# A planned order of 840 tasks is written anew, two more blocks of y are turned by DMA, and the idle matmuls multiply zeros by zeros

## The chip, the cores and the metric

The kernel runs on one core of a Trainium2 chip. The metric is the device time of one execution in microseconds (us). Lower is better. All times in this document are device times or times inside a profiled execution, counted from the start of its span.

## The reference

The program is a gated linear recurrence followed by a two-layer network with a SiLU. Four sequences of 768 steps with 8 heads of width 48 go through the recurrence. Its output, 3072 rows of 384, goes through a 384 x 2048 matrix, SiLU and a 2048 x 384 matrix.

```python
f = 1.0 / (1.0 + np.exp(-f_logit))
for t in range(S):                                   # S = 768
    state = f[:, :, t, :, None] * state + np.einsum('bhd,bhe->bhde', k[:, :, t], v[:, :, t])
    y[:, :, t] = np.einsum('bhd,bhde->bhe', q[:, :, t], state)
x = y.transpose(0, 2, 1, 3).reshape(B * S, H * D)    # 3072 x 384
h = x @ w_in                                         # w_in 384 x 2048
out = (h / (1.0 + np.exp(-h))) @ w_out               # w_out 2048 x 384
```

## The kernel before

A sequence is cut into six chunks of 128 steps, so that there are 24 blocks (sequence, chunk). `PAIRS` joins them into twelve pairs, numbered 0 to 11, each with two blocks, 0 and 1. Pairs 0 to 3 (kind 'T') hold the first two chunks of one sequence, interleaved by step. Pairs 4 to 11 (kind 'N') hold the same chunk of two sequences. A chunk needs the state that the chunk before it left.

The work on a pair is split into small tasks. A task has a kind, a pair and mostly a block, so `sc.7.0` is the score task of block 0 of pair 7:

- `f`, `k`, `q`, `v` load a pair's inputs. `wi` and `wo` (four of each, on the POOL queue) load a quarter of the first and the second matrix, lines 206 and 209.
- `E` and `L` make the logarithm of the gate on ACT, `cs` sums it over the steps by matmul (lines 304 to 314), `ia`, `a` and `al` take exponentials of the sums (line 316 and its neighbours), and `ki` and `qg` multiply k and q by them (line 321).
- `tq` turns the products on the tensor engine (line 328), and `qkc` copies them out of PSUM. In pairs 4 to 11 `qkD` does both by a transposing DMA on the SP queue (line 336).
- `sc` makes the scores (lines 345, 349), `at` masks them (line 353), `y` applies them to v and adds the state's part (lines 262, 361, 365), `yi` is the state's part alone in block 1 of a 'T' pair.
- `d`, `sd` and `su` (lines 274 or 382, 386, 392) carry the state forward. `vb` casts v.
- `yc` copies y out of PSUM. Then `yT` turns it by three matmuls with an identity (line 373) and `xc` copies the result into the tile xT. Or `yD` does both by one transposing DMA on the SP queue (line 377).
- `mi` (line 248) is one eighth of the first matrix product for a pair, six matmuls of width 256. `si` (line 253) is the SiLU of it. `mo` (line 285) is a quarter of the second product for a block, four matmuls of width 384. `oc` copies the result out of PSUM, `so` stores it.

There is no scheduler at build time. The text `PLAN` is a table of about 840 words, made by a planner outside the kernel; the kernel issues the tasks in the order of the words. A word is `task:engine:buffers`. The engine is A (ACT, the scalar engine), V (DVE, the vector engine), G (POOL), S (the SP queue) or P (the tensor engine, PE). The buffers are the numbers of the tiles that the task opens, out of `SLOTS`: eight PSUM banks `pb`, four `f`, six each of `k`, `q`, `v`, and so on. So the table fixes, for each engine, the order in which it takes its instructions; what an engine waits for follows from the data and from the buffers. An engine stands still at an instruction whose inputs are not there, and everything behind it stands too. The SP queue is such an engine as well: nearly all DMAs are issued by it in the order of the table.

Words `idle.W.n` are n matmuls of width W whose result nobody reads; they fill the tensor engine's time in the opening. The first four loads of the table are issued ahead of everything else, before the constants are made. ACT has two tables of functions, one for exponentials and logarithms, one for SiLU, and a table is loaded (line 484) wherever the table of tasks changes from one to the other.

Of the kernel before, what the change touches and what calls it, by code (L numbers as in the profile page):

```python
# [43 lines left out]
v.0.0:S:4 d.1:P:2,7 at.1.0.0:V: idle.512.5::3 y.1:P:4,3 qg.0.0:G: qg.0.1:V:2 wi.0:G: L.2.0:A:1 tq.0.0:P:6 q.2.0:S:4 k.2.0:S:3 cs.2.0:P:5 ki.0.1:V:
sd.1.0:A:0 tq.0.1:P:2 al.0:A:0 su.1.0:G:0 cs.2.1:P:1 yc.1.0:A:2 yT.1.0:P:0 qkc.0.0:V:0 qkc.0.1:V: ia.2.0:A:1 xc.1.0:V:3 yi.1.1:P: a.2.0:A:4 wi.2:G:
vb.0.0:V:1 sc.0.1:P:2,4 v.2.0:S:5 a.2.1:A:0 yc.1.1:A:0 vb.0.1:G:3 al.2:A:4 idle.256.1::6 yT.1.1:P:6 ia.2.1:A:2 sc.0.0:P:5,1 d.0:P:3,0 at.0.1.1:V:1
at.0.1.0:V: xc.1.1:A: mi.1.2:P:4 at.0.0.1:V:2 mi.1.3:P:6 at.0.0.0:V: y.0:P:5,1 yc.0.0:V:2 sd.0.0:A:0 su.0.0:G:0 yi.0.1:P: wo.0:G: wo.1:G: mi.1.6:P:2
si.1.3:A:0 f.3.0:S:3 sd.1.1:V:1 yc.0.1:A:1 yT.0.0:P:5 yT.0.1:P:6 xc.0.1:V:1 mi.1.7:P:3 xc.0.0:A: si.1.7:A: si.1.2:A: sd.0.1:V:0 f.5.0:S:2 si.1.6:A:
mi.0.3:P:5 mi.0.0:P:0 mi.0.2:P:7 mi.0.7:P:4 mi.0.1:P:6 mi.1.4:P:1 mi.1.5:P:3 si.1.4:A: si.0.1:A:1 ki.2.0:V:1 mi.0.5:P:2 si.0.0:A: mi.1.0:P:6 si.0.5:A:
mi.0.4:P:0 mi.1.1:P:1 si.1.5:A: si.0.2:A: si.1.0:A: si.1.1:A: mo.0.1.0:P:2 mo.0.0.0:P:3 wo.2:G: mo.1.0.0:P:7 mi.0.6:P:6 si.0.6:A: mo.1.1.0:P:1  # L50
si.0.3:A: si.0.7:A: ki.2.1:G:4 mo.1.0.1:P: qg.2.1:V: qg.2.0:V: mo.1.1.1:P: mo.0.1.1:P: tq.2.0:P:4 qkc.2.0:V:1 tq.2.1:P:6 mo.0.0.1:P: wo.3:G: si.0.4:A:
qkc.2.1:V: mo.1.1.2:P: sc.2.1:P:6,4 sc.2.0:P:0,5 at.2.0.0:V:0 at.2.0.1:V: mo.1.0.2:P: mo.0.0.2:P: at.2.1.0:V:1 at.2.1.1:V: mo.0.1.2:P: mo.0.1.3:P:
vb.2.0:G:0 vb.2.1:A:1 d.2:P:6,5 su.0.1:G:0 sd.2.0:V:0 y.2:P:4,0 mo.1.1.3:P: oc.0.1:V:0 mo.0.0.3:P: E.3.0:A:1 L.3.0:A:1 cs.3.0:P:2 yc.2.0:V:1 E.5.0:A:0
L.5.0:A:0 a.3.0:A:4 su.2.0:G:0 sd.2.1:V:0 q.5.0:S:0 yi.2.1:P: yc.2.1:A:0 yT.2.0:P:4 cs.3.1:P:6 al.3:A:0 ia.3.1:A:1 cs.5.0:P:5 xc.2.0:V:0 a.5.0:A:0
cs.5.1:P:0 k.3.0:S:0 ki.3.1:G:0 yT.2.1:P:4 xc.2.1:V: oc.0.0:A:1 q.3.0:S:1 mo.1.0.3:P: oc.1.0:A:2 oc.1.1:V:3 qg.3.0:V:1 mi.2.6:P:4 al.5.1:A:2
qg.5.0:V:2 k.5.1:S:1 a.5.1:A:1 mi.2.0:P:1 mi.2.1:P:7 mi.2.2:P:3 q.5.1:S: qg.5.1:V:3 ia.5.1:A:2 al.5.0:A:3 a.3.1:A:4 qg.3.1:V: k.5.0:S: ia.5.0:A:0
# [51 lines left out]
def kernel(  # L108
# [32 lines left out]
    buf = {}  # L141
# [290 lines left out]
    def run(kind, rest, eng, got):  # L432
        if kind == "idle":
            for _ in range(rest[1]):
                nc.tensor.matmul(buf["pb", int(got)][:, 0:rest[0]], triu, zero[:, 0:rest[0]], start=True, stop=True, skip_group_check=True)  # L435
            return
# [80 lines left out]
```

## Time and profile before

| | us |
|---|---|
| median of three runs | 181.32 |
| the three runs | 177.69, 181.32, 600.86 |
| the profiled execution, its own time | 175.95 |
| its span in the trace | 174.2 |
| outside the span | 1.75 |
| PE busy in the span | 168.2 (97%) |
| ACT busy | 128.6 (74%) |
| DVE busy | 81.5 (47%) |
| POOL busy | 63.4 (36%) |

The busy time of an engine is the time in which an instruction of its own runs, without waiting, branching or issuing of DMAs. The ends of matmuls are modelled. The granted clock of the tensor engine stands at full in all slices. DMA shares are the mean over 16 DMA engines of the time that packets took, and they can be above one in a short stretch. A chain of waits is followed back from the last instruction to what released it.

### The profile page before, as it was taken

To read this page: it belongs to the slowest core of one execution; us is meant where nothing else is said; L and a number is where in the kernel's file an instruction comes from. 1 tells how busy PE (TensorE), PEld (TensorE's weight loads), DVE (VectorE), ACT (ScalarE), POOL (GpSimd) and SP (SyncE) were. 2 spreads that over 40 slices of the span, in tenths; PEclk is the share of its full clock that TensorE was granted. 3 is DMA by queue.
4 is the path that set the end of the run, shared out by engine and by line. 5 is a ranking of instruction groups with operands and counts; after the bars stand their busy time and mean duration, and the time that the engine had idled before them with its cause. 6 is when DMAs were issued, how large, how long until landed. Compare 5 with 4: busy or idle time off the path is not lost.

```text
span 174.2 us, 4746 instructions
## 1 busy us (share of the span) xinstructions
PE 168.2 (97%) x1927; PEld 125.2 (72%) x1927; DVE 81.5 (47%) x166; ACT 128.6 (74%) x237; POOL 63.4 (36%) x106
## 2 busy tenths in 40 slices
PE   6889999999999999999999999999999999999992
PEld 2456888666876888766787687786697686886872
DVE  7389713267858762126686176045760152520101
ACT  3879839665999989997499688999589574281630
POOL 6088612312583357400737235400470970000000
PEclk9999999999999999999999999999999999999999
DMA  5999999999899998999999895969979998222202
GB/s 143 323 322 210 214 224 204 229 184 263 191 202 182 213 198 179 222 191 212 177 222 177 162 224 131 221 133 226 224 145 186 202 198 226 49 72 108 90 4 90
DMA packets 110677, 32.12 MB, mean 184 GB/s; under 512 B 104096, under 2 KB 110528, under 8 KB 110656
## 3 DMA queue, kind: packets, MB, share of 16 engines
q1 hardware_dynamic: 106048, 27.76, 75.7%
q0 software_dynamic: 3936, 3.74, 12.1%
q10 hardware_dynamic: 672, 0.33, 0.6%
q8 instruction: 15, 0.25, 0.6%
q14 instruction: 6, 0.05, 0.1%
HBM read 25.17 MB, written 4.72 MB: 172 GB/s over the span
## 4 chain that ended last, share of the span: by engine, by line
PE 85%; ACT 7%; DVE 2%; DMA 2%; issue 1%; ACTq 0%
PE pb L285 35%; PE pb L248 32%; ACT hT L253 3%; PE pb L349 3%; ACT L484 2%; PE pb L361 2%; PE pb L328 2%; DMA f<-in_f_logit_dram 2%; PE pb L365 2%; PE pb L373 2%; PE pb L311 2%; PE pb L345 1%; ACT x L316 1%; PE pb L382 1%; PE pb L262 1%; DVE atm L353 1%
## 5 line engine op out<-in xcount | busy, mean ns | idle before, releaser
L248 PE MATMUL pb<-xT,w_in_sb 128*128 128x256 bf16 x576 | 69.5, 272 | 0.2 <-ACT hT L253 0.2
L285 PE MATMUL pb<-w_out_sb,hT 128*128 128x384 bf16 (+2 forms) x400 | 68.7, 320 | 0.0
L248 PEld LDWEIGHTS <-w_in_sb 128*128 128x128 bf16 x576 | 54.7, 98 | 9.1 <-issue 0.7
L253 ACT ACTIVATE hT<-pb 128x512 bf16<-128x512 f32 x96 | 50.5, 609 | 14.4 <-PE pb L248 14.1
L285 PEld LDWEIGHTS <-hT 128*128 128x128 bf16 x400 | 37.2, 98 | 20.3
L392 POOL TENSOR_TENSOR st<-sd,al 48x192 bf16<-48x192 f32 x40 | 21.9, 549 | 48.4 <-PE pb L361 34.1
L316 ACT ACTIVATE x<-pb 128x384 f32<-128x384 f32 x48 | 21.4, 499 | 5.8 <-PE pb L304 2.5
L353 DVE TENSOR_TENSOR atm<-pb,triu 128x512 bf16<-128x512 f32 x32 | 20.1, 684 | 11.2 <-PE pb L349 6.6
L484 ACT ACT_TABLE_LOAD x17 | 21.8, 1283 | 0.3
L183 DVE COPY ob<-pb 128x384 f32<-128x384 f32 (+1 forms) x11 | 5.7, 528 | 27.3 <-PE pb L285 27.3
L321 POOL TENSOR_TENSOR qk<-k,x 128x384 bf16<-128x384 f32 x12 | 13.0, 1094 | 12.8 <-DMA k<-in_k_dram 9.7
L386 DVE TENSOR_TENSOR sd<-pb,st 128x384 f32<-128x384 f32 x16 | 8.8, 552 | 11.5 <-PE pb L382 10.6
L321 POOL TENSOR_TENSOR qk<-q,x 128x384 bf16<-128x384 f32 x11 | 10.9, 997 | 8.5 <-ACT x L316 7.9
L233 ACT ACTIVATE e<-f 128x768 f32<-128x768 f32 x12 | 10.1, 842 | 3.8 <-DMA f<-in_f_logit_dram 3.7
L181 ACT COPY ob<-pb 128x384 f32<-128x384 f32 (+1 forms) x14 | 6.7, 476 | 8.3 <-PE pb L285 8.1
L321 DVE TENSOR_TENSOR qk<-q,x 128x384 bf16<-128x384 f32 x13 | 9.0, 710 | 5.8 <-ACT x L316 5.7
L321 DVE TENSOR_TENSOR qk<-k,x 128x384 bf16<-128x384 f32 x12 | 8.0, 677 | 6.7 <-DMA k<-in_k_dram 6.6
L353 DVE TENSOR_TENSOR atm<-pb,mask 128x512 bf16<-128x512 f32 x16 | 10.0, 684 | 1.6 <-PE pb L345 1.6
L183 DVE CAST yb<-pb 128x384 bf16<-128x384 f32 x13 | 7.1, 555 | 6.7 <-ACT hT L253 3.1
L183 POOL CAST vb<-v 128x384 bf16<-128x384 f32 x13 | 7.0, 542 | 8.4 <-DMA v<-in_v_dram 8.0
L435 PE MATMUL pb<-zero,triu 128*128 128x512 bf16 (+1 forms) x26 | 7.5, 424 | 1.4 <-POOL triu masks.py:66 1.4
L181 ACT CAST yb<-pb 128x384 bf16<-128x384 f32 x11 | 5.3, 488 | 4.3 <-PE pb L365 4.3
(70 smaller groups left out, 138.9 us busy)
## 6 DMA issues: line engine op xcount, KB each, us to landing
f<-in_f_logit_dram SPq DMA_DIRECT2D x11, 384.0 KB, 5.5
k<-in_k_dram SPq DMA_DIRECT2D x10, 384.0 KB, 5.5
q<-in_q_dram SPq DMA_DIRECT2D x10, 384.0 KB, 4.6
v<-in_v_dram SPq DMA_DIRECT2D x10, 384.0 KB, 5.0
out_dram<-ob SPq DMA_DIRECT2D x13, 192.0 KB, 2.1
w_in_sb<-in_moe_w_in_dram POOLq DMA_DIRECT2D x4, 384.0 KB, 8.7
w_out_sb<-in_moe_w_out_dram POOLq DMA_DIRECT2D x4, 384.0 KB, 9.7
out_dram<-ob SPq DMA_DIRECT2D x14, 96.0 KB, 3.4
```

The costliest lines, as they stand in the source:

```text
L181: nc.scalar.copy(dst, src)
L183: ENG[eng].tensor_copy(dst, src)
L233: return nc.scalar.activation(e, at("f", P)[:, j * w:(j + 1) * w], AF.Exp, scale=-1.0)
L248: nc.tensor.matmul(h[:, i, cols], w_in_sb[:, kk, n * 128:(n + 1) * 128], at("xT", P)[:, kk, cols], start=(kk == 0), stop=(kk == KT - 1))
L253: return nc.scalar.activation(at("hT", P)[:, 2 * j:2 * j + 2, :], at("h", P, j).rearrange("p (n c) -> p n c", n=2), AF.Silu)
L285: nc.tensor.matmul(at("o" + key, P, i)[:, 0:cols.stop - cols.start], at("hT", P)[:, n, i * C:(i + 1) * C], w_out_sb[:, n, cols], start=(n ...
L316: nc.scalar.activation(at(kind, P, i).rearrange("p h d -> p (h d)"), at("cs", P, i)[:, 0:HD], AF.Exp, scale=1.0 if kind == "ia" else -1.0)
L321: ENG[eng].tensor_mul(at("qk", P, i)[:, j, :, 0:D], heads("qk"[j], P, i), at("ia" if j else "a", P, i))
L353: ENG[eng].tensor_mul(at("atm", P, i)[:, r], at(f"s{r}", P, i).rearrange("p (n c) -> p n c", c=C), mask[:, None, :].to_broadcast([C, NP, C]))
L386: nc.vector.tensor_add(at("sd", P, i), d_ps, prev_state(P, i))
L392: nc.gpsimd.tensor_mul(at("st", P, i)[lo:lo + D, :, r * D:(r + 1) * D], at("sd", P, i)[lo:lo + D, :, r * D:(r + 1) * D], al_of(P, i)[lo:lo ...
L484: nc.scalar.preload_act_table_set(turns[n])
```

## The change

Three things are changed, and nothing else in the kernel.

1. `PLAN` is a new table. The same tasks stand in a new order, on partly other engines and in other buffers. The planner that wrote it counts fetches of instructions when it estimates when transfers land. Of the two ways to turn y, 13 blocks take `yT` where 15 did, and 11 take `yD` where 9 did: blocks `6.1` and `9.1` go over from `yT` and `xc` to `yD`.
2. The idle matmuls read the tile `zero` as both operands. Before, the stationary operand was the triangle `triu`, which POOL makes; `zero` is filled by DVE.
3. Of the `idle` words, the second run of width 512 has four matmuls in place of five, and a third run of five has become one. The rest stand in about the same places.

```diff
-f.1.0:S:0 k.1.0:S:4 idle.512.10::4 q.1.0:S:1 f.0.0:S:1 f.1.1:A: E.1.0:A:0 L.1.0:A:0 idle.512.1::0 idle.256.1::0 cs.1.0:P:6 a.1.0:A:2 cs.1.1:P:0
+f.1.0:S:3 k.1.0:S:3 q.1.0:S:1 f.1.1:A: f.0.0:S:0 idle.512.10::7 E.1.0:A:0 L.1.0:A:2 idle.512.1::0 idle.256.1::0 cs.1.0:P:4 a.1.0:A:1 v.1.0:S:3
...
-                nc.tensor.matmul(buf["pb", int(got)][:, 0:rest[0]], triu, zero[:, 0:rest[0]], start=True, stop=True, skip_group_check=True)
+                nc.tensor.matmul(buf["pb", int(got)][:, 0:rest[0]], zero[:, 0:C], zero[:, 0:rest[0]], start=True, stop=True, skip_group_check=True)
```

The new order is shown at three places, by the instructions that stand in a row on an engine.

The first place is POOL in the opening, from the third and fourth quarter of `w_in` on. `qk...<-q` is `qg`, `qk...<-k` is `ki`, `st` is `su`, and `w_out_sb` is `wo`. Before:

```order
L206 DMA w_in_sb_161<-in_moe_w_in_dram 128x3x512
L183 CAST vb3_101<-v4_81 128x384
L392 TENSOR_TENSOR st00_148<-sd0_126,al0_128 48x4x48 x2
L209 DMA w_out_sb_162<-in_moe_w_out_dram 128x4x384 x3
L321 TENSOR_TENSOR qk4_97<-k3_68,x2_90 128x8x48
L209 DMA w_out_sb_162<-in_moe_w_out_dram 128x4x384
```

And now:

```order
L183 CAST vb2_100<-v1_78 128x384
L206 DMA w_in_sb_161<-in_moe_w_in_dram 128x3x512
L392 TENSOR_TENSOR st00_148<-sd1_127,al3_131 48x4x48 x2
L209 DMA w_out_sb_162<-in_moe_w_out_dram 128x4x384
L392 TENSOR_TENSOR st10_149<-sd0_126,al4_132 48x4x48 x2
L321 TENSOR_TENSOR qk1_94<-q2_73,x0_88 128x8x48
L209 DMA w_out_sb_162<-in_moe_w_out_dram 128x4x384 x2
L321 TENSOR_TENSOR qk2_95<-q2_73,x4_92 128x8x48
L321 TENSOR_TENSOR qk2_95<-k3_68,x1_89 128x8x48
L209 DMA w_out_sb_162<-in_moe_w_out_dram 128x4x384
```

The second and third quarter of `w_out` were issued right behind the first; now they stand behind `su.1.1` and `qg.2.0`, and `qg.2.0` waits for the load `q.2.0`. The last quarter of `w_in` has moved behind a cast that waits for `v.0.0`.

The second place is the SP queue around the transposes of pairs 6 and 7. `qkT` is `qkD`, `xT` is `yD`. Before:

```order
L227 DMA f0_61<-in_f_logit_dram 128x16x48
L296 DMA out_0_dram<-ob3_137 64x384 x2
L336 DMA_TRANSPOSE qkT0_105<-qk3_96 128x8x128
L377 DMA_TRANSPOSE xT1_119<-yb1_116 128x3x128
L336 DMA_TRANSPOSE qkT2_107<-qk1_94 128x8x128
L227 DMA k1_66<-in_k_dram 128x16x48
```

And now:

```order
L227 DMA f2_63<-in_f_logit_dram 128x16x48
L296 DMA out_0_dram<-ob1_135 64x384 x2
L336 DMA_TRANSPOSE qkT3_108<-qk2_95 128x8x128
L336 DMA_TRANSPOSE qkT2_107<-qk1_94 128x8x128
L377 DMA_TRANSPOSE xT0_118<-yb2_117 128x3x128
L377 DMA_TRANSPOSE xT0_118<-yb0_115 128x3x128
L227 DMA k5_70<-in_k_dram 128x16x48
```

The two `qkD` of pair 7 now follow each other, and both `yD` of pair 6 stand behind them, where one `yD` stood between them.

The third place is PE ahead of the scores of pair 7 (line 349). Line 285 is `mo`, 311 `cs`, 382 `d`, 248 `mi`. Before:

```order
L285 MATMUL pb0_140<-w_out_sb_162,hT1_123 128x384
...
L311 MATMUL pb4_144<-lf0_85,triu_152 128x384
...
L382 MATMUL pb1_141<-vb2_100,qk1_94 128x96
...
L311 MATMUL pb6_146<-lf0_85,triu_152 128x384
...
L285 MATMUL pb3_143<-w_out_sb_162,hT1_123 128x384
...
L248 MATMUL pb1_141<-xT1_119,w_in_sb_161 128x256
...
L349 MATMUL pb0_140<-qkT0_105 128x128
```

And now:

```order
L285 MATMUL pb2_142<-w_out_sb_162,hT1_123 128x384
L311 MATMUL pb4_144<-lf2_87,triu_152 128x384
...
L382 MATMUL pb0_140<-vb3_101,qk2_95 128x96
...
L349 MATMUL pb7_147<-qkT3_108 128x128
...
L349 MATMUL pb5_145<-qkT2_107 128x128
...
L285 MATMUL pb2_142<-w_out_sb_162,hT1_123 128x384
```

`cs.8.1`, `d.7.1`, the last quarter of `mo.4.1` and the first `mi` of pair 6 stood ahead of the scores of pair 7; now the scores come first.

More of the change, by code (lines that the diff above doesn't have):

```diff
@@ L44 @@
[L44 to L55, printed above, removed]
@@ new lines @@
+mi.2.6:P:7 ki.3.1:V: al.5.0:A:4 al.5.1:A:2 ia.5.1:A:4 ki.3.0:V: tq.3.1:P:5 tq.3.0:P:3 mi.2.7:P:6 f.4.0:S:2 si.2.1:A:0 si.2.0:A: ki.5.1:V:4 mi.2.2:P:1
+v.5.1:S:5 qg.5.0:V:3 qkc.3.0:V:1 qkc.3.1:V: mi.2.5:P:3 si.2.4:A: si.2.6:A: si.2.3:A: si.2.5:A: mo.2.1.0:P:5 d.3:P:0,2 sc.3.1:P:4,3 ki.5.0:V: si.2.2:A:
+at.3.1.0:V:1 sc.3.0:P:7,1 qkD.5.0:S:2 si.2.7:A: at.3.0.1:V:0 qg.5.1:G: at.3.1.1:V: sd.3.0:A:0 mo.2.1.1:P: qkD.5.1:S:3 mo.2.1.2:P: mo.2.1.3:P:
+mo.2.0.0:P:0 mo.2.0.1:P: v.5.0:S: E.6.0:A:0 su.3.0:G:0 sd.3.1:V:0 oc.2.1:V:5 at.3.0.0:V: E.4.0:A:1 L.4.0:A:0 sc.5.0:P:5,3 L.6.0:A:1 su.0.1:G:0
```

110 lines of the change are left out of this document (59 added, 51 removed).

## The prediction

> **What bounds the kernel now.** First the page: the span, how busy the engines are, and the chain that ended last.
>
> ```profile
> span 174.2 us, 4746 instructions
> PE 168.2 (97%) x1927; PEld 125.2 (72%) x1927; DVE 81.5 (47%) x166; ACT 128.6 (74%) x237; POOL 63.4 (36%) x106
> PE 85%; ACT 7%; DVE 2%; DMA 2%; issue 1%; ACTq 0%
> ```
>
> The tensor engine (PE) is busy nearly throughout and carries 85% of the chain. Where it is not, the view by stretches of time tells.
>
> ```profile
> core 0: us, PE busy (x) PEld busy (x) DVE busy (x) ACT busy (x) POOL busy (x), PEclk, DMA share, GB/s
> 0.00:18.20 18.20, 15.55 (x233) 9.25 (x234) 13.41 (x44) 13.02 (x26) 10.59 (x29) 1.00 1.03 248
> 18.20:62.00 43.80, 43.77 (x598) 33.49 (x595) 25.25 (x45) 34.58 (x67) 16.95 (x26) 1.00 1.10 208
> 62.00:74.00 12.00, 11.83 (x105) 9.79 (x103) 3.33 (x8) 11.77 (x21) 7.51 (x10) 1.00 1.02 209
> 74.00:150.00 76.00, 76.00 (x808) 56.04 (x806) 35.46 (x65) 59.24 (x105) 28.37 (x41) 1.00 0.94 189
> 150.00:171.10 21.10, 21.08 (x195) 16.59 (x193) 3.79 (x7) 10.02 (x19) 0.00 (x0) 1.00 0.18 57
> ```
>
> Three things are to be seen. From 18.2 us to 171.1 us PE stands still for 0.03 + 0.17 + 0.02 = 0.22 us in all, so a new order finds almost nothing there to remove. In the opening, PE is idle for 2.65 us and otherwise holds filler, so an order could win there. And the DMA engines are as full as PE until 150 us (shares 0.94 to 1.10): the loads keep pace with PE, but not by much. So PE's work sets the end, and DMA is a second limit close behind.
>
> **The opening, 0 to 18.2 us.** In the chain of waits it is a ladder over three engines:
>
> ```profile
> 7.61 1.51 DVE qk L321 x3
> 9.17 0.64 PE pb L328 x8
> 9.83 0.70 DVE qkTT L183
> 10.57 0.44 PE pb L345 x16
> 13.58 0.57 PE pb L262 x32
> 14.71 0.33 PE pb L304 x2
> 18.25 1.42 PE pb L248 x12
> L183 DVE CAST vb<-v 128x384 bf16<-128x384 f32 x6 | 2.5, 428 | 8.0 <-DMA v<-in_v_dram 8.0
> ```
>
> The new table puts `vb.1.0` on DVE between the two `qkc` of pair 1, so the copy at 9.83, the scores at 10.57 and `y` at 13.58 come up to 0.43 us later (one such cast, mean 428 ns). `al.1` leaves the place ahead of the exponentials on ACT, which wins under 0.1 us. `cs.2.0`, which stood behind `y.1` (14.71, 0.33 us), goes ahead of it, into time in which PE only filled. So the first `mi` (18.25) moves by +0.43 - 0.1 - 0.33 = 0.0 us. Five idle matmuls fewer cost or win nothing: they stood in such waits. Zeros for both operands let the filler start before the triangle is ready, but the first real matmul waits for the gate's load and logarithm whenever the filler starts. The bounds for the opening are -1.7 us (two thirds of the 2.65 us idle) and +0.5 us (the cast is paid whole and a little more).
>
> ACT loads two more tables in the new order (one exponential now stands between the first SiLUs):
>
> ```profile
> L484 ACT ACT_TABLE_LOAD x17 | 21.8, 1283 | 0.3
> L253 ACT ACTIVATE hT<-pb 128x512 bf16<-128x512 f32 x96 | 50.5, 609 | 14.4 <-PE pb L248 14.1
> ```
>
> That is 2 x 1.283 = 2.6 us of ACT at about 22 us. It is hidden as long as PE finds free PSUM banks, since the SiLUs wait 14.1 us in all for PE, not PE for them. Without that cover it would cost at most 1 us, as eight banks let PE run on for some `mi` first. I take nothing.
>
> **The weights on POOL.** `wo.1` and `wo.2` now stand behind `qg.2.0`, and that waits for `q.2.0`:
>
> ```profile
> 10.18 1.29 SPq L227 DMA_DIRECT2D q<-in_q_dram  x1
> DMA to landing us min/median/max: 3.5/6.9/12.8
> L321 POOL TENSOR_TENSOR qk<-q,x 128x384 bf16<-128x384 f32 x11 | 10.9, 997 | 8.5 <-ACT x L316 7.9
> 19.95 2.29 POOL L209 DMA_DIRECT2D w_out_sb<-in_moe_w_out_dram  x3
> DMA to landing us min/median/max: 7.8/9.7/13.3
> 21.52 7.92 PE pb L248 x72
> 32.05 2.60 PE pb L285 x16
> ```
>
> (The landing rows are of `q` from 8 to 40 us, and of `w_out_sb`.) By the longest landing `q.2.0` is there at 10.18 + 12.8 = 23.0, `qg.2.0` ends at 24.0, and `wo.1` is issued then, where it was issued at 20.7. It lands at 31.8, 33.7 or 37.3 by shortest, median and longest. PE needs it at the first second-quarter `mo`: from 18.25 on there stand 16 `mi` (0.66 each, 7.92/12), four `mo` (0.65, 2.60/4), and about 2.1 us of one `y` (0.57 at 13.58), two `tq` (0.64 at 9.17) and smaller ones, which makes 33.5. By the median that is a wait of 0.2 us, and I take that; the bounds are 0 and 3.8 us. For the low end speaks that `wo.0`, issued ahead of it as before, keeps the POOL queue's transfers going meanwhile, so that `wo.1` need not land later than it did. What is queued behind the waiting `qg.2.0` on POOL is exactly `wo.1`, `wo.2`, `qg.2.1` and `ki.2.1`.
>
> **Two blocks of y by DMA.** Three transposes of a block take this on PE:
>
> ```profile
> 93.25 0.17 PE pb L373 x3
> ```
>
> Two blocks are 0.34 us of PE, which is on the path, so -0.34 us; their copies were on engines with slack. The Trainium skill (TensorE: Matmul & The Clock Gate, Part 4) gives about 275 ns for one transpose within a kernel; by that figure six would be 1.65 us. The row shows them pipelined at 0.06 us each, and the row decides. What replaces them is a transposing DMA on SP each, and the time that this needs before `mi` can start:
>
> ```profile
> 92.39 1.61 SPq L336 DMA_TRANSPOSE qkT<-qk  x1
> 94.12 1.19 SPq L377 DMA_TRANSPOSE xT<-yb  x1
> 95.40 1.25 SPq L336 DMA_TRANSPOSE qkT<-qk  x1
> DMA to landing us min/median/max: 3.1/3.6/5.4
> DMA to landing us min/median/max: 2.3/2.3/4.2
> 99.32 0.82 PE L248 MATMUL pb<-xT,w_in_sb 128*128 128x256 bf16 x6
> 100.07 0.62 PE L349 MATMUL pb<-qkT 48*128 48x128 bf16 x16
> ```
>
> (The first landing row is that of `qkT`, the second that of `xT`.) This is the place in the new order that is tightest. Now, the second `qkD` of pair 7 is issued at 95.40 and lands at 99.0 by the median, 1.1 us ahead of the scores at 100.07. In the new order it goes ahead of the `yD`, so it is issued at about 94.12 and lands at 97.7. But PE arrives earlier too: one `mo` quarter (0.65), one `mi` (0.66), and a `cs`, a `d` and a `yT` (0.6 together, an estimate by the row of 0.17) no longer stand ahead, 1.9 us, so it is there at 98.15, or 97.9 with the stalls of before gone. Slack 0.2 to 0.4 us. Behind them the two `yD` are issued at 95.4 and 96.7 and the second lands at 99.0. The first `mi` of pair 6 is reached at 97.9 plus 0.55 for the scores (0.62 with its end) and 0.9 for the rest of `mo.4.1` and `cs.8.1`, 99.35. I take 0.1 us of wait; the bounds are 0 and, with the longest landings of the rows (5.4 and 4.2), 1.9 us.
>
> **The end.**
>
> ```profile
> 171.12 0.29 DVE ob L183
> L181 ACT COPY ob<-pb 128x384 f32<-128x384 f32 (+1 forms) x14 | 6.7, 476 | 8.3 <-PE pb L285 8.1
> out_dram<-ob SPq DMA_DIRECT2D x13, 192.0 KB, 2.1
> out_dram<-ob SPq DMA_DIRECT2D x1, 64.0 KB, 1.6
> ```
>
> The last matmuls were those of a third of block 11.0, with a short copy on DVE (0.29) and a store of 64 KB (1.6). Now `mo.10.1` is last, whole: a copy on ACT (0.48) and a store of 192 KB (2.1). That is +0.19 and up to +0.5; the DMA engines are idle there, so I take +0.5 in all, between +0.2 and +0.7.
>
> **The sum**, against the profiled execution's own 175.95 us (span 174.2 and 1.75 around it): opening 0.0, yT -0.34, the 0.17 us that PE stood still between 62 and 74 us (ACT has three copies and casts fewer there, and its ten SiLUs start earlier) -0.17, wait at pair 7 +0.1, weights +0.2, end +0.5. Together +0.29: **176.2 us**. The median of the three runs shown, 181.32, and even the fastest, 177.69, lie above the profiled execution, by 5.4 and 1.7 us; so the range has to hold that too.
>
> **Rivals.** *The weights come late* (slower). Place: PE at the second quarter of `mo.0.0`. It decides when the landing of `wo.1` takes over 9.5 us from 24.0. At the longest landing seen, 13.3 us, PE waits 3.8 us, of which nothing comes back, as PE is full to the end: 176.2 - 0.2 + 3.8 = 179.8. For it: the DMA share is 1.10 there. Against it: the queue's transfers go on without a gap.
>
> *PE outruns the transposes* (a little slower). With the longest landings at pair 7 the wait is 1.9 us, 178.0. For it: the new order brings PE to these tiles some 2 us earlier while the loads ahead of them are the same, and adds two transposes to full DMA engines. Against it: in the row of before most land within 3.6 us.
>
> *The opening gets shorter* (faster). If the ladder loses 1.7 us, no landing costs anything, and the end only 0.2, it is 176.2 - 1.7 - 0.3 - 0.3 = 173.9. Nothing shown gives 3.5 us, since PE's own work after 18.2 us stays.
>
> *Zeros do not wake the clock.* In the opening the filler's weight loads stand like this:
>
> ```profile
> 3.48 0.15 PEld L435 LDWEIGHTS <-triu 128*128 128x128 bf16 x1 [0.28 <-issue]
> 3.90 1.04 PEld L435 LDWEIGHTS <-triu 128*128 128x128 bf16 x5 [0.28 <-issue]
> ```
>
> Until 3.90 they are 0.42 us apart, then about 0.21: PE becomes twice as fast while only filler runs. If zero weights did not do that, the real matmuls from 6.0 to about 17 us would run at half speed; those of the ladder above and the six steps between 13.58 and 17 would cost 1.1 + 3.0 = 4 us, 180.3. Against it: the moving operand was all zeros already. The Trainium skill (TensorE: Matmul & The Clock Gate, Part 1) says that a gate opens after a window of about 3.4 us in which PE was busy; by that rule zeros do as well as anything. The trace agrees as far as it goes, with 2.5 us from 1.37 to 3.90.
>
> **Chances.** My sum, within about 1 us: 0.62. Transposes 0.17, weights 0.10, opening 0.08, clock 0.03. A measurement of this kernel can hardly tell 2% (3.5 us) from no change. The sum, the opening and nearly all of the transposes lie within 2%. Slower by more: weights 0.08 of its 0.10, clock 0.03, and 0.02 of the transposes, 0.13. Faster by more: 0.05, for a gain in the opening or in waits that PE's modelled ends hide. Within: 0.82. The range reaches from the opening's case, 173.9, to the weights' case (179.8) and the clock's (180.3), 180.2; that also holds the sum with the 1.7 us by which the fastest plain run stands above the profile.
>
> **What would show it.** The profile of the changed kernel should have PE idle for under 3 us before its first line 248, which starts at 18.0 to 18.7 us; line 373 with six matmuls fewer; 19 table loads; a first line 285 at about 30 us without a gap in the five after it; and no gap of PE over 0.3 us after 20 us, the scores of pair 7 at 97.5 to 98.5 us. The last PE instruction should end at 170.5 to 171 us, and the store after it should take 2.2 to 2.7 us to land. A PE gap of a microsecond or more at any line 285, 349 or 248 proves the sum wrong at that term; an opening shorter by over 1.7 us proves the ladder wrong.

## The result, and the profile after

The changed kernel took 178.69 us (median of 20 runs, 177.54 to 180.57), the kernel before 178.68 (median of 20, 176.55 to 600.86). The two medians are alike because the kernel before has more disturbed executions among its 20 (one of the kind is shown below, with a bad opening); with these left out on both sides, as in every ratio below, the ratio is 1.0061, with a 95% interval of 1.0033 to 1.0089. The change is within 2%, and a little slower. The prediction said 176.2 us, a ratio of 176.2 / 175.95 = 1.0014.

The profiled execution took 179.10 us, with a span of 177.3. First the page of the changed kernel: span, PE, the granted clock in 40 slices, and the chain by engine.

```profile
span 177.3 us, 4719 instructions
PE 169.0 (95%) x1916; PEld 125.5 (71%) x1916; DVE 81.4 (46%) x168; ACT 130.9 (74%) x238; POOL 59.1 (33%) x103
PEclk9999999999999999999999879999999999999999
PE 69%; DMA 11%; SPq 6%; ACT 5%; POOL 4%; issue 3%; DVE 0%; POOLq 0%; ACTq 0%
```

PE carried 85% of the chain and now carries 69%; DMA and the SP queue carry 17%. And the clock, at full in every slice before, falls in the slices from 97.5 to 106 us. The stretches, with the same borders as before except at the end:

```profile
0.00:18.20 18.20, 15.47 (x229) 8.93 (x230) 13.66 (x45) 13.44 (x27) 10.27 (x28) 1.00 1.04 250
18.20:62.00 43.80, 43.80 (x590) 33.46 (x589) 22.30 (x41) 37.18 (x70) 19.31 (x29) 1.00 1.07 206
62.00:74.00 12.00, 12.00 (x114) 10.00 (x112) 3.14 (x7) 11.55 (x20) 3.25 (x5) 1.00 1.06 202
74.00:150.00 76.00, 74.06 (x781) 54.80 (x779) 38.14 (x70) 58.70 (x104) 26.01 (x42) 0.98 0.94 185
150.00:174.00 24.00, 23.70 (x212) 18.26 (x210) 4.11 (x8) 9.62 (x20) 0.31 (x1) 1.00 0.30 85
```

(Columns: stretch, its length, busy time of PE, PEld, DVE, ACT and POOL with instructions, granted clock, DMA share, GB/s.) Up to 74 us all is as forecast or better. From 74 to 150 us PE stands for 76.00 - 74.06 = 1.94 us, where it stood for nothing before. The waits of PE and its instructions around 100 us show where:

```profile
PE pb L349 <- DMA qkT<-qk: 1.9, 1, 1.9
...
97.29 0.40 PE L349 MATMUL pb<-qkT 48*128 48x128 bf16 x8
99.61 0.40 PE L349 MATMUL pb<-qkT 48*128 48x128 bf16 x8 [1.92 <-DMA qkT<-qk]
...
101.02 3.69 PE L248 MATMUL pb<-xT,w_in_sb 128*128 128x256 bf16 x18
```

PE comes to the scores of pair 7 at 97.29 us, and stands between the scores of its two blocks until the transposed q and k of 7.1 are there. Then 18 matmuls of line 248 take 3.69 us. In another execution of the same kernel, below, the same 18 take 2.13. So 1.9 us are lost in the wait, and about 1.6 behind it, while the clock is down. The SP queue of the changed kernel, and one row of the kernel before:

```profile
88.53 1.73 SPq L227 DMA_DIRECT2D f<-in_f_logit_dram  x1
90.36 3.50 SPq L296 DMA_DIRECT2D out_dram<-ob  x2
94.04 3.10 SPq L336 DMA_TRANSPOSE qkT<-qk  x2
97.24 2.50 SPq L377 DMA_TRANSPOSE xT<-yb  x2
```

```profile
89.65 2.13 SPq L296 DMA_DIRECT2D out_dram<-ob  x2
```

The two parts of the store of block 3.1 hold SP for 3.50 us, where they held it for 2.13; the first transpose of pair 7 is issued at 94.04, where it was issued at 92.39. In the chain the second one runs from 95.89 for 3.67 us, so it lands at 99.56, against 95.40 and 98.64 before. It comes 0.9 us later, and PE 2.8 us earlier (97.29 for 100.07). The store isn't all of the delay: SP came to it at 90.36, where it came at 89.65.

### The profile page after: what moved, and what is told of

Its sections match the earlier page's. It is cut to its first block, busy times and chain, and to the rows that moved or that the text cites. A ratio compares the mean times of both kernels' runs of the same rounds, so it can differ in the third digit from the quotient of the medians.

```text
span 177.3 us, 4719 instructions
## 1 busy us (share of the span) xinstructions
PE 169.0 (95%) x1916; PEld 125.5 (71%) x1916; DVE 81.4 (46%) x168; ACT 130.9 (74%) x238; POOL 59.1 (33%) x103
## 4 chain that ended last, share of the span: by engine, by line
PE 69%; DMA 11%; SPq 6%; ACT 5%; POOL 4%; issue 3%; DVE 0%; POOLq 0%; ACTq 0%
PE pb L248 30%; PE pb L285 26%; DMA k<-in_k_dram 3%; POOL qk L321 2%; DMA q<-in_q_dram 2%; SPq L336 2%; DMA qkT<-qk 2%; DMA f<-in_f_logit_dram 2%; DMA xT<-yb 2%; PE pb L328 2%; PE pb L349 1%; SPq L227 1%; ACT e L233 1%; PE pb L304 1%; ACT lf L237 1%
## 5 line engine op out<-in xcount | busy, mean ns | idle before, releaser
L285 PE MATMUL pb<-w_out_sb,hT 128*128 128x384 bf16 (+2 forms) x400 | 69.7, 320 | 0.0
L248 PEld LDWEIGHTS <-w_in_sb 128*128 128x128 bf16 x576 | 55.7, 99 | 8.7 <-DMA xT<-yb 0.3
L392 POOL TENSOR_TENSOR st<-sd,al 48x192 bf16<-48x192 f32 x40 | 21.1, 528 | 35.3 <-DVE sd L386 14.3
L183 DVE COPY ob<-pb 128x384 f32<-128x384 f32 (+1 forms) x15 | 7.8, 535 | 28.6 <-PE pb L285 28.4
L321 POOL TENSOR_TENSOR qk<-k,x 128x384 bf16<-128x384 f32 x10 | 10.5, 1055 | 30.0 <-DMA k<-in_k_dram 15.2
L321 DVE TENSOR_TENSOR qk<-k,x 128x384 bf16<-128x384 f32 x14 | 8.9, 650 | 15.6 <-DMA k<-in_k_dram 7.1
L353 DVE TENSOR_TENSOR atm<-pb,mask 128x512 bf16<-128x512 f32 x16 | 10.1, 684 | 5.0 <-PE pb L345 5.0
L321 DVE TENSOR_TENSOR qk<-q,x 128x384 bf16<-128x384 f32 x15 | 10.1, 681 | 4.5 <-ACT x L316 2.8
L321 POOL TENSOR_TENSOR qk<-q,x 128x384 bf16<-128x384 f32 x9 | 9.3, 1035 | 6.1 <-DMA q<-in_q_dram 5.3
L181 ACT COPY ob<-pb 128x384 f32<-128x384 f32 (+1 forms) x10 | 4.7, 470 | 7.0 <-PE pb L285 5.2
L435 PE MATMUL pb<-zero 128*128 128x512 bf16 (+1 forms) x21 | 6.9, 473 | 1.2 <-DVE halves L467 1.2
```

The source lines that it names most:

```text
L181: nc.scalar.copy(dst, src)
L183: ENG[eng].tensor_copy(dst, src)
L248: nc.tensor.matmul(h[:, i, cols], w_in_sb[:, kk, n * 128:(n + 1) * 128], at("xT", P)[:, kk, cols], start=(kk == 0), stop=(kk == KT - 1))
L285: nc.tensor.matmul(at("o" + key, P, i)[:, 0:cols.stop - cols.start], at("hT", P)[:, n, i * C:(i + 1) * C], w_out_sb[:, n, cols], start=(n ...
L321: ENG[eng].tensor_mul(at("qk", P, i)[:, j, :, 0:D], heads("qk"[j], P, i), at("ia" if j else "a", P, i))
L353: ENG[eng].tensor_mul(at("atm", P, i)[:, r], at(f"s{r}", P, i).rearrange("p (n c) -> p n c", c=C), mask[:, None, :].to_broadcast([C, NP, C]))
```

## The experiments

All runs are set against the kernel before on the same chip. "Idle" is the time for which PE stood between 74 and 150 us in the profile, 1.94 us in the changed kernel, 0.00 before.

### The wait itself: the store ahead of it, filler in it, the operands, the end

**The store of 3.1 goes from SP to POOL,** behind `ki.7.1` there.

```diff
-so.3.1:S:
+so.3.1:G:
```

> The changed kernel with one store task moved: so.3.1 (two DMAs) leaves the SP queue, where it took 3.5 us just ahead of the transposes of pair 7, and is issued by POOL behind ki.7.1. Theory Q (the queue): the wait of PE at the scores of pair 7 (2.1 us at line 349) comes from what stands ahead of the transposes on SP; without it the wait falls under 0.3 us, the slow stretch of matmuls behind it (213 ns in place of 109, some 3 us) goes too, and the time falls by 1 to 2 us against the changed kernel, to a ratio of 0.994 to 1.000 against the kernel before. Theory D (the DMA engines are full): the stores' bytes still go over the same 16 engines, the transposes land at the same time and the wait stays at 1.5 to 2.1 us; ratio 1.003 to 1.009.

177.71 us, ratio 1.0037 (0.9997 to 1.0077). The stretch, the waits and SP in this run:

```profile
74.00:150.00 76.00, 73.54 (x785) 54.32 (x784) 37.82 (x70) 58.89 (x105) 27.52 (x44) 1.00 0.97 191
...
PE pb L248 <- DMA xT<-yb: 2.1, 3, 0.9
PE pb L349 <- DMA qkT<-qk: 0.3, 1, 0.3
...
91.09 5.21 SPq L336 DMA_TRANSPOSE qkT<-qk  x2
```

The wait at the scores is gone but for 0.3 us, and the idle time is larger than before, 2.46 us: PE now waits three times for y (`xT`), at most 0.9 us each. But the clock stays at 1.00. The ratio is lower than the changed kernel's 1.0061, with intervals that overlap; that one wait of 2 us costs more than three of up to 0.9 fits this, and isn't shown by the times alone.

**Nine idle matmuls of width 512 ahead of the scores of pair 7.**

```diff
+idle.512.9::7
 sc.7.0:P:7,3 sc.7.1:P:5,6
```

> The changed kernel with nine idle matmuls of width 512 added on PE just ahead of the scores of pair 7 (about 1.95 us at full clock, into the wait of 2.1 us). Theory C (the clock): the wait lets the clock of PE fall, and the slow matmuls behind it cost up to 1.6 us in the runs in which that happens; with the filler the mean granted clock stays at 1.00 and line 248 behind the wait runs at 109 ns; ratio 0.998 to 1.004. Theory W (the wait alone counts): the clock falls in the profile by chance and the time doesn't change; ratio 1.003 to 1.009.

178.47 us, ratio 1.0077 (1.0033 to 1.0120). PE is busy for 75.37 of the 76 us and the clock is at 0.996 or more in all 12 executions, but no time is won. The filler takes 1.9 us in every execution, also where the transposes would have landed in time: the median of 178.47 lies between those of the changed kernel with the fall of the clock and without it (179.26 and 177.98, below). This holds the clock, and shows nothing else.

**The triangle as the stationary operand of the idle matmuls again.**

```diff
-zero[:, 0:C], zero[:, 0:rest[0]]
+triu, zero[:, 0:rest[0]]
```

> The changed kernel with the triangle as stationary operand of the idle matmuls again, as before. Theory of the record (zeros cost and win nothing): no difference from the changed kernel, ratio 1.003 to 1.009; the filler runs at half speed from its start until some point between 3 and 6 us, which moves from run to run. Theory Z (zeros wake the clock later): with the triangle the clock is full by 4 us as before, the opening ends 0.3 us or more earlier, ratio under 1.003.

178.93 us, ratio 1.0075 (1.0023 to 1.0127); idle 1.62 us. In its profile, as in the changed kernel's, the filler's weight loads stand 0.42 us apart until about 5.2 us and closer behind that. No difference that the operands make is to be seen.

**The end in the order of before** (10.1, then 11.1, then the halves of 11.0). In this kernel the store of block 4.1 stands behind the copy that takes its buffer, so these 128 rows hold another block's data; the same bytes are moved.

```diff
-... so.10.0 ... mo.11.0.2.0 mo.11.1.* ... mo.10.1.* oc.10.1 ... so.10.1
+... so.10.0 mo.10.1.* oc.10.1 so.10.1 ... mo.11.1.* ... mo.11.0.2.0 ... so.11.0.1
```

> The changed kernel with the last tasks in the order of before: the four quarters of mo.10.1 go ahead, and the last matmuls are the third of block 11.0, with a copy on DVE and a store of 64 KB. Theory E (the end): what follows the last matmul shortens by 0.3 to 0.7 us, ratio 0.999 to 1.006. Theory without E: the end costs the same whichever store is last, ratio 1.003 to 1.009.

178.21 us, ratio 1.0052 (1.0012 to 1.0092), idle 2.21 us with the fall of the clock. The end isn't where the loss is.

### Is it SP's standing still at 48 us, or the two added transposes of y?

In 50 to 57 us the DMA share fell from 0.98 (before, first row) to 0.71 (changed, second row), since SP stands from 48.35 to 50.83 us at the transpose of 5.0, which waits for VectorE. The third row is of the run after the next.

```profile
50.00:57.00 7.00, 6.97 (x91) 4.48 (x88) 4.37 (x8) 6.92 (x12) 3.17 (x7) 1.00 0.98 180
```

```profile
50.00:57.00 7.00, 7.00 (x134) 4.72 (x132) 4.93 (x10) 6.80 (x11) 2.02 (x4) 1.00 0.71 144
```

```profile
50.00:57.00 7.00, 6.99 (x101) 4.58 (x100) 4.87 (x9) 6.64 (x11) 2.02 (x4) 1.00 1.03 172
```

**Four transfers go ahead of that transpose.**

```diff
+v.5.0:S: so.1.1:S: k.4.1:S:3 q.6.0:S:0
 qkD.5.0:S:2 ... qkD.5.1:S:3
-v.5.0:S: ... so.1.1:S: ... k.4.1:S:3 ... q.6.0:S:0
```

> The changed kernel with four words moved on SP: the loads of v.5.0, k.4.1 and q.6.0 and the store of 1.1 stand ahead of the DMA transpose of 5.0, at which SP stands from 48.35 to 50.83 us waiting for VectorE. Theory G (the 2.5 us in which SP hands out nothing leave the 16 DMA engines at a share of 0.71 in 50-57 us, against 0.98 before, and are never made up, so every later transpose lands late): the share in 50-57 rises to 0.9 or more, the scores of pair 7 wait under 0.6 us instead of 2.1, PE's idle time in 74-150 falls from 1.9 us to under 0.7, and the ratio comes to 0.995 to 1.002. Theory Y (the two added DMA transposes of y, with their 256-byte packets, are what the engines can't carry): idle time in 74-150 stays at 1.5 to 2.5 us, ratio 1.004 to 1.009.

181.35 us, ratio 1.0234 (1.0180 to 1.0288). SP and the wait:

```profile
49.81 2.97 SPq L296 DMA_DIRECT2D out_dram<-ob  x2
...
54.25 4.14 SPq L336 DMA_TRANSPOSE qkT<-qk  x2
...
PE pb L349 <- DMA qkT<-qk: 3.8, 3, 3.0
```

Neither theory saw this. With the transfers ahead of it, the transpose is issued at 54.25 instead of 50.83, and the scores of pair 5 wait 3.0 us; the clock falls there too. The gap couldn't be filled from behind without making the transpose late.

**VectorE makes its operand first.** This fills the gap from the other side.

```diff
+ki.5.0:V:
 qkc.3.0:V:1 qkc.3.1:V: ...
-ki.5.0:V:
```

> The changed kernel with one word moved on VectorE: the product for k of 5.0 (ki) stands ahead of the two copies of pair 3's transposed q and k (1.27 us), so that the DMA transpose of 5.0, at which SP stands until 50.83 us, can be issued some 1.2 us earlier, with the five transfers behind it. Theory G (SP's gap there is what makes the later transposes late): DMA share in 50-57 rises from 0.71 to 0.8 or more, the wait at the scores of pair 7 falls from 2.1 us to 0.9 or less, ratio 1.000 or less. Theory L (the engines' load up to there decides, wherever the queue stands still; the transposes are late because PE comes to the scores 2.8 us earlier than before): the wait stays at 1.5 to 2.3 us, ratio 1.003 to 1.008.

177.90 us, ratio 1.0048 (1.0020 to 1.0076). The share in 50 to 57 us is 1.03 (third row above), so the gap is filled; the idle time is 2.32 us, and the longest wait at pair 7 is still 1.1. The first transpose of pair 7 is issued at 94.42 us, no earlier than the 94.04 of the changed kernel. SP's gap isn't the cause.

**y of 6.1 is turned by TensorE again** (9.1 stays with the DMA).

```diff
-yD.6.0:S:0 ... yD.6.1:S:
+yT.6.1:P:6 ... xc.6.1:V:0 ... yD.6.0:S:
```

> The changed kernel with y of unit 6.1 turned by TensorE and copied by VectorE again, as before (one DMA transpose less on SP; 9.1 stays on DMA). Theory Y (the added DMA transposes are the cost): PE's idle time in 74-150 falls below 0.7 us and the ratio to 1.001 or less. Theories G and L: the transposes of pair 7 stand ahead of this one on SP, so the wait at their scores stays at 1.5 to 2.3 us, and the ratio at 1.004 to 1.008.

177.31 us, ratio 1.0006 (0.9983 to 1.0029). Most of the loss is gone, as the theory of the added transposes had it; but the profile doesn't show what that theory expects:

```profile
74.00:150.00 76.00, 73.93 (x797) 54.87 (x795) 39.32 (x73) 58.41 (x104) 26.23 (x42) 1.00 0.97 189
...
PE pb L248 <- DMA xT<-yb: 1.1, 1, 1.1
PE pb L349 <- DMA qkT<-qk: 1.0, 1, 1.0
```

PE stands for 2.07 us, as long as in the changed kernel, but in pieces of 1.1 us and less, and without a fall of the clock in this execution (three of the 12 had a granted clock under 0.996).

**The same two blocks by DMA in the order of before.**

```diff
-yT.6.1:P:1 ... xc.6.1:V:1 ... qkD.7.0 ... yD.6.0:S: ... qkD.7.1
+qkD.7.0 yD.6.1:S:1 yD.6.0:S: ... qkD.7.1
-yT.9.0 yT.9.1:P:7 ... xc.9.0:V:0 xc.9.1:V: ... qkD.8.1
+yT.9.0 yD.9.1:S:0 ... xc.9.0:V: ... qkD.8.1
```

> The kernel before with one part of the change alone: y of units 6.1 and 9.1 turned by DMA instead of TensorE (two words yT and xc less each, one word yD more), all else in the order of before. Theory G (SP's gap at 48-51 us, which this kernel doesn't have): DMA has room for it; PE's idle time in 74-150 stays under 0.5 us and the ratio is 0.996 to 1.001, since six transposes leave PE. Theory Y (the added DMA transposes): the scores of pair 7 or the tiles behind the y of unit 6 wait 1 us or more, and the ratio is 1.003 to 1.008.

181.46 us, ratio 1.0219 (1.0166 to 1.0272). SP, what it waited for, and PE:

```profile
124.13 1.19 SPq L377 DMA_TRANSPOSE xT<-yb  x1
125.41 1.26 SPq L336 DMA_TRANSPOSE qkT<-qk  x1
...
SPq L377 <- DVE yb L183: 3.6, 1, 3.6
...
128.54 1.03 PE L349 MATMUL pb<-qkT 48*128 48x128 bf16 x16 [2.36 <-DMA qkT<-qk]
129.50 2.51 PE L248 MATMUL pb<-xT,w_in_sb 128*128 128x256 bf16 x12
```

SP stands 3.6 us at the y of 9.1, and the q and k of 8.1 behind it are issued at 125.41 instead of 119.7. PE waits 2.36 us for them, and the clock falls again: 12 matmuls of line 248 take 2.51 us, 0.21 each, against 0.12 each in the 2.13 us for 18 shown below. This is the price of a place in SP's queue, paid by what stands behind a waiting transpose.

A further run moved the two words behind `qkD.7.1` and `qkD.8.1` of before; there the first matmuls of pair 6 came ahead of the transpose of 6.1, so these read another pair's rows and SP had to wait for them.

> The kernel before with y of 6.1 and 9.1 turned by DMA, as in the run that put these two ahead of the q and k transposes of pair 7 and of 8.1, but now behind them on SP. There the transpose of 8.1 was issued at 125.4 us instead of 119.7, since SP stood at the y of 9.1 waiting for its copy. Theory P (the place in SP's queue cost it, not the bytes): qkD of 8.1 is issued by 121 us again, no wait over 1 us at its scores, ratio 0.998 to 1.005. Theory Y (the added transfers cost it wherever they stand): waits of 1 us or more in 98-134 stay, ratio 1.010 to 1.022.

It took 186.45 us (182.25 to 189.44 in six executions), and no ratio is on record. In its profile the clock fell in the opening as well. It decides nothing.

### How much is load, and what before does by itself

**The kernel before once more, by itself.**

> The kernel before once more, unchanged, as a run of its own: how far two runs of one kernel stand apart, and a second profiled execution beside the one of 175.95 us. Theory G and theory Y: ratio 0.997 to 1.003, and again no wait of PE over 0.5 us in 74-150. Theory N (the base of the prediction was one lucky execution; others of before lose as much at transposes that land late as the changed kernel does): the profile shows waits at lines 349 or 248 of together 1 us or more in 74-150, and an own time of 177 or more.

Ratio 1.0001 (0.9953 to 1.0048). Its profile fell on an execution of 182.70 us:

```profile
10.21 6.88 DMA q<-in_q_dram
...
0.00:24.00 24.00, 17.94 (x207) 10.73 (x212) 13.70 (x42) 12.71 (x26) 11.02 (x29) 0.87 1.02 236
...
74.00:150.00 76.00, 75.83 (x788) 56.77 (x786) 33.94 (x62) 63.40 (x111) 31.40 (x45) 1.00 0.96 185
```

Here the load of q for pair 0 lands late, at 17.09 us (12.6 in the profile of 175.95), and the clock falls in the opening. From 74 us on nothing is lost but 0.17 us. So the mid waits belong to the changed kernel, and the theory that before has them too falls. But the base was lucky in another way: 175.95 us is close to the shortest time that before showed in any job (175.88); the median of its executions at a granted clock of 0.996 or more was 176.9 to 177.5 in the six later jobs.

**Either kernel without the stores of 0.1, 1.1, 2.1, 3.0 and 3.1** (these rows of the output aren't written).

```diff
-so.0.1:S: ... so.1.1:S: ... so.2.1:S: ... so.3.0:S: ... so.3.1:S:
```

> The changed kernel without the five stores of 0.1, 1.1, 2.1, 3.0 and 3.1 (these rows of the output are never written), so that SP issues five transfers fewer and the DMA engines carry about 1 MB less between 50 and 94 us. If DMA (engines or SP's queue) is what the tiles of 74-150 us wait for, by theory G as by theory Y: no wait over 0.5 us at the scores of pair 7, PE's idle time in 74-150 under 0.6 us, time 1.5 to 3 us under the changed kernel's, ratio to before 0.988 to 0.999. If it is another engine's order (theory O: VectorE, ScalarE or POOL bring the operands late): the waits stay, idle time 1.5 or more, ratio 1.003 to 1.008.

> The kernel before without the five stores of 0.1, 1.1, 2.1, 3.0 and 3.1 (these rows of the output are never written), to stand beside the changed kernel without them, which took 0.991 of before. Theory L (the new order is shorter on TensorE, by the yT and the stall of my sum, and is held up by DMA alone): before has no wait there to lose, so its ratio stays at 0.997 to 1.001, 0.6 to 1% above that of the changed kernel without them. Theory O (the new order gains nothing on TensorE; stores cost either kernel the same): ratio 0.988 to 0.994.

The changed kernel without them: 175.50 us, ratio 0.9908 (0.9873 to 0.9944). Before without them: 176.55 us, ratio 0.9954 (0.9918 to 0.9991). The stretch in both, in this order:

```profile
74.00:150.00 76.00, 76.00 (x828) 56.90 (x827) 41.19 (x74) 59.99 (x107) 27.44 (x44) 1.00 0.98 183
```

```profile
74.00:150.00 76.00, 75.83 (x796) 56.07 (x795) 34.43 (x63) 61.23 (x109) 29.02 (x42) 1.00 0.89 177
```

With 1 MB less to carry the changed kernel has no wait left, and comes out about 1 us under before without them. So transfers are what holds up the new order. That it is also the shorter one on TensorE fits, by the 0.5 us of the sum's terms for `yT` and the stall; the rest isn't separated from the opening, since in the profile of before without these stores (178.08 us) PE also stood for 1.05 us between 18.2 and 74 us, and for nothing there in the other. The two intervals just meet, so the size of that 1 us is rough.

### The wait that comes and goes

**The changed kernel once more.**

> The changed kernel once more, unchanged, beside the two above. Theory C (what makes it slower is that its wait of 2 us at the scores of pair 7 is long enough for TensorE's clock to fall, which puts about 1.6 us on top): executions with the fall (granted clock about 0.99) stand 1 to 1.6 us above those without, and the profile, if the clock is 0.99, shows matmuls at 213 ns behind the wait, and if it is 1.00, a wait of under 1.9 us there. Ratio 1.003 to 1.009.

179.12 us, ratio 1.0104 (1.0033 to 1.0176, from few runs). The profiled execution took 176.62 us, with a clock of 1.00:

```profile
89.44 2.35 SPq L296 DMA_DIRECT2D out_dram<-ob  x2
91.97 3.55 SPq L336 DMA_TRANSPOSE qkT<-qk  x2
...
97.33 0.62 PE L349 MATMUL pb<-qkT 48*128 48x128 bf16 x16
...
99.99 2.13 PE L248 MATMUL pb<-xT,w_in_sb 128*128 128x256 bf16 x18 [1.03 <-DVE atm L353]
```

The same table, and here the store holds SP for 2.35 us instead of 3.50, the transposes are issued 2.1 us earlier, and the scores of pair 7 don't wait; one wait of 1.03 us behind them is left. That is the spread of the kernel: over both jobs 11 of its 26 executions ran at a granted clock under 0.996, and their median is 179.26; 14 at 0.996 or more have 177.98 (one more took 433.91). The 1.3 us between them are what was expected of the fall.

The same count over the other kernels tells which ones have the fall. With the store of 3.1 ahead of the transposes of pair 7 on SP and nothing to fill the wait (the changed kernel, triangle, end of before, VectorE first, 6.1 or both blocks of pair 6 on TensorE) it is 34 of 80 executions. With that store moved or left out, or the wait filled (six kernels, some of them below), it is 1 of 66. The count doesn't say where the clock fell. The kernel before has it too, in 26 of its 152 executions of these jobs and with a median of 182.6 us; where one of them was profiled, above, it was in the opening.

### Mending it

**Three stores go behind the transposes that stood behind them,** and 6.1 stays on TensorE as in the run above. From here on the table takes one line more, so that lines stand one higher (249 for 248, 350 for 349).

```diff
-so.3.1:S: ... qkD.7.0:S:3 qkD.7.1:S:2
+qkD.7.0:S:3 qkD.7.1:S:2 so.3.1:S:
-so.5.1:S: yD.7.1:S:1 ... qkD.9.1:S:0 yD.7.0:S:
+yD.7.1:S:1 ... yD.7.0:S: so.5.1:S: qkD.9.1:S:0
-so.7.0:S: ... yD.8.0:S:1 ... yD.8.1:S:
+yD.8.0:S:1 ... yD.8.1:S: so.7.0:S:
```

> The changed kernel with y of 6.1 turned by TensorE (ratio 1.0006 by itself), and three stores moved on SP behind the DMA transposes that stood behind them: that of 3.1 behind both q and k transposes of pair 7, that of 5.1 (with the q and k transpose of 9.1) behind the y of 7.0, that of 7.0 behind the y of 8.1. The bytes are the same. Theory S (the stores' place ahead of the transposes on SP makes them late): qkD of 7.1 is issued by 93 us and lands by 96.5, the scores of pair 7 wait under 0.3 us, idle time of PE in 74-150 falls from 2.1 us to under 1, ratio 0.992 to 0.998. Theory L (the engines are full up to there; a store that is behind only makes other transfers late, as when that of 3.1 went to POOL): idle time stays at 1.3 to 2.5 us, spread over other tiles, ratio 0.998 to 1.004.

177.72 us, ratio 1.0037 (0.9994 to 1.0080). The scores of pair 7 wait 0.2 us only, and 1.1 us are waited for y of 6.0 right behind them; idle 1.35 us. The wait has gone to the next tile, and the ratio is no better than the 1.0006 with 6.1 alone.

**And the end in the order of before**, now with the store of 4.1 ahead of the copy that takes its buffer.

> As the run before, and the last three units stored in the order of the kernel before (10.1, then 11.1, then the halves of 11.0), the store of 4.1 ahead of the copy that takes its buffer. If the last store of a whole 192 KB block behind the last matmuls costs what my sum said (0.5 us, 0.2 to 0.7): ratio 0.001 to 0.004 under the run before. If the end is set elsewhere: within 0.001 of it.

177.02 us, ratio 0.9989 (0.9950 to 1.0028). The medians fall by 0.7 us, and the ratio by 0.0048 with intervals that overlap; the term of the end (0.5 us, 0.2 to 0.7) fits, without being proved. Its waits:

```profile
PE pb L249 <- DMA xT<-yb: 1.3, 2, 1.1
...
PE pb L350 <- DMA qkT<-qk: 0.3, 1, 0.3
```

**And y of 6.0 by TensorE**, so that nothing of block 6 waits for a transfer behind pair 7.

```diff
-yD.6.0:S:
+yT.6.0:P:0 ... xc.6.0:V:
```

> As the run with three stores behind the transposes and the end of before, and y of 6.0 turned by TensorE as well (three transposes of 0.056 us and one copy more on VectorE, one DMA transpose less): at 99.55 us PE waited 1.1 us there for this transfer. Theory L (the DMA engines' load is the limit): the wait at the first line-249 tile behind the scores of pair 7 goes, idle time of PE in 74-150 falls from 2.2 us to 1.2 or less, ratio 0.990 to 0.996. If the wait only goes to the next tile behind a transfer: idle time 1.6 or more, ratio 0.996 to 1.001.

175.70 us, ratio 0.9897 (0.9863 to 0.9930): faster than both kernels, all 12 executions at a clock of 0.997 or more, between 175.03 and 176.44 us.

```profile
PE 90%; ACT 3%; DVE 2%; DMA 2%; issue 1%; DVEq 0%; ACTq 0%
...
90.22 5.12 SPq L337 DMA_TRANSPOSE qkT<-qk  x2
95.86 1.12 SPq L297 DMA_DIRECT2D out_dram<-ob  x2
...
L337 SPq DMA_TRANSPOSE qkT<-qk x2: 1232/2464/3696, 90.2 to 94.1; - x2
...
74.00:150.00 76.00, 76.00 (x831) 56.93 (x829) 40.89 (x76) 59.26 (x107) 27.12 (x43) 1.00 0.98 189
```

The first transpose of pair 7 is issued 3.8 us earlier than in the changed kernel, the store behind them, and PE doesn't stand at all between 74 and 150 us. The second one, for which PE had waited, goes out at 94.11 us, only 1.8 us earlier than the 95.89 of the changed kernel. For the first now holds SP for 3.70 us (fourth row: the shortest, median and longest issue in ns, then the first and last start), where it took 1.25 behind the store. In these profiles of the new order SP was held at this place for 2.35 to 3.75 us, by whichever entry stood there. In the four runs with the store of 3.1 moved the second transpose goes out at 94.1 to 94.9 us; in the eight profiles with the store ahead (without the run that moved four transfers), at 94.25 to 96.6. And PE comes to these scores 1 us later than in the changed kernel, at 98.25 us. The DMA share is 0.98, so the engines are as full as ever: it is the order in which they are filled that counts, once the one transfer too many is off the path.

**Which of the edits?** Both blocks of pair 6 on TensorE, with the stores and the end of the changed kernel:

> The changed kernel with one edit alone: y of both 6.0 and 6.1 turned by TensorE and copied by VectorE; stores and end stand as in the changed kernel. If the transfers awaited behind pair 7 are the loss (theory L): PE's idle time in 74-150 falls to 1.0 us or less and the ratio to 0.992 to 0.997, the rest to the run that also moved stores and the end (0.990) being the end's term of up to 0.5 us. If the stores' place on SP was needed as well: a wait of 1 us or more at the scores of pair 7, ratio 0.998 to 1.002.

180.37 us, ratio 1.0100 (1.0019 to 1.0182); SP has 3.75 us of store at 90.81 again, the scores of pair 7 wait 1.4 us in the profile, and 4 of the 6 executions ran at a clock under 0.99. The interval is wide, but the profile has the long store and the wait again. So the turn alone wasn't enough here, and the store's place seems to be needed too; what the end adds to the 1% isn't separated. And the turn of 6.0 in the order of before:

> The kernel before with y of 6.0 turned by TensorE (three transposes more there, one DMA transpose less). Before has no wait of PE over 0.33 us between 74 and 150 us in its profile, so if the waits are what the new order brought (theory L): nothing to win, 0.17 us more on PE, ratio 0.998 to 1.003. If a DMA transpose of y less wins in any order: ratio 0.990 to 0.996.

177.97 us, ratio 1.0040 (1.0003 to 1.0077): no faster, and in the profile PE has the three transposes more and a wait of 0.5 us for the copy ahead of them. So the 1% belongs to the new order, with its transfers put right.

## Why the prediction was wrong, point by point

**The opening, 0.0 us.** Right within 0.2 us; its three terms weren't measured one by one. The first line 248 starts at 18.07 us in the chain, for 18.25: 0.18 us won. The two more table loads cost nothing: there is no gap of PE after 18.2 us up to 74.

**The weights, +0.2 us.** The low end came. The first line 285 is at 29.95 us without a gap behind it. The rival that they come late (0.10) didn't come.

**Two blocks of y, -0.34 us, and the stall at 62 to 74 us, -0.17.** Line 373 has 39 matmuls, 6 fewer; the stall is gone (12.00 of 12.00 us). The price of what replaces them was put at the transposes' issue and landing behind pair 7, and so it stands in the next term.

**The wait at pair 7, +0.1 us (0 to 1.9).** This is the step that failed. Its arrival of PE was about right: 97.9 forecast, 97.29 measured. Its landing wasn't. The step took the time at which SP comes to the first transpose, 92.39 us, from the profile of before, and only moved the second one up behind it, to 94.12; it landed by that at 97.7. Measured are 94.04 and 95.89, and a landing at 99.56. The queue ahead of the transposes was taken as fixed, though the whole table is new: the store of 3.1 ahead of them held SP for 3.50 us, and in the execution without a wait 2.35; SP also came to that store 0.7 us later than before. The bound of 1.9 us was met by luck. From the step's own numbers the longest landings give 94.12 + 5.4 - 97.9 = 1.6 us, and the wait came from a late issue and not from a long landing. And the step knew only the wait, not that the clock falls behind it: 1.6 us more.

**The end, +0.5 us (0.2 to 0.7).** The last PE instruction ends at 173.95, and 179.10 - 173.95 = 5.15 us lie behind it; before it was 175.95 - 171.08 = 4.87. So +0.3 for the copy and store, within the bounds.

**The sum.** With what was measured: -0.18 - 0.34 - 0.17 + 1.94 + 1.6 + 0.25 (PE's standing after 150 us, 24.00 - 23.70 less the 0.05 to the last matmul's end) + 0.3 = +3.4, so 179.4 for an execution that took 179.10; 0.3 us aren't explained.

**The rivals.** "PE outruns the transposes" (0.17, 178.0 us, a wait of 1.9) came at its place and with its size, and the fall of the clock on top, but not by its mechanism, the longest landings. What was held against it, that most transposes land within 3.6 us, was true and beside the point: this one took 3.67, but was issued 1.8 us late. Zeros open the clock as well as the triangle does, as far as the run with the triangle can tell.

**The base.** Of the 2.5 us between forecast and median, 1.1 are the base: the profiled execution of before stood at 175.95 where the median of its executions at a granted clock of 0.996 or more is about 177.1. I had seen that the fastest plain run stood 1.7 us above it and widened the range for it, but not moved the forecast. The range, 173.9 to 180.2, holds the result. In the ratio, which the base doesn't touch, 1.0014 was forecast, and 1.0061 came.

## What to carry to other kernels

When an order is written anew, price each wait on a transfer by the queue that now stands ahead of it, entry by entry, and not by when the old queue came to it; with DMA engines at a share near 1.0 an entry ahead (here a store of two parts of 96 KB) took 2.35 or 3.50 us from one execution to the next, so a slack under a microsecond is none. Look which single transfers PE waits for, and put those ahead of stores, or off the DMA where TensorE does them for 0.06 us a piece; it takes all of them at one place, since the wait goes to the next as long as one is left. And take the base from several executions.

## What the runs showed of the hardware that I had not expected

A single wait of TensorE of about 2 us can be followed by 3.4 us at half speed, and in these profiles shorter ones weren't. In the middle of the kernel, waits of up to 1.42 us left the clock at 1.00. Waits of 1.92 and 2.05 us (the changed kernel, and the one with the end of before), 2.36 us (the two blocks by DMA in the order of before) and 2.98 us (four transfers ahead) were followed by a granted clock of 0.50 and matmuls at about twice their time, each time for 3.413 us; so was one of 1.85 us in the run that decides nothing. The stretch doesn't start with the wait: after the wait of 1.92 us the next matmuls still ran at full speed (those of line 349 took 0.40 us, as ahead of it), and the clock fell at about 100.85 us, 1.2 us after PE had gone on; at the wait of 2.36 us it fell 0.3 us before PE went on. The Trainium skill (TensorE: Matmul & The Clock Gate, Part 1) has the clock go down after an idle window of about 3.4 us, which runs freely. The traces agree with the window: from its first rise to its next fall the clock stood at full for 95.57, 95.57, 122.88 and 54.61 us in these four, which is 28, 28, 36 and 16 times 3.413 us. That 1.92 us were enough doesn't fit an idle time of 3.4 us, and here the measurement decides. In the 3.41 us ahead of the four falls after these waits PE stood for 1.9 to 2.6 us, so a window that is idle in part seems to be enough; what share it takes wasn't measured. It would also fit that only some executions have the fall, as a wait of 2 us can lie in one window or be shared by two; no run tests this.

And the same issue of the same store took SP 2.35 us in one execution and 3.50 in another, with everything behind it moved by as much or more. Where the store was moved away, the transpose that took its place held SP for 3.2 to 3.7 us instead. What SP waits for there stays open: the profile names a SiLU of ScalarE at the store, on which it doesn't depend.
